# A scan and gated-MLP kernel: four of the first block's twelve hidden units move from whole fp32 products to three rounded passes, with a new start and load order

## The chip, the core and the metric

The kernel runs on one core of a Trainium2 chip. The metric is device time in microseconds (us): the median of the runs before the change is 351.71 us (351.47 to 352.11, 3 runs).

## What is computed

The first half is a gated linear scan over 768 positions for 4 batches and 8 heads, in chunks with decays that are products of `clip(a, 1e-6, 1)`. Its output, 3072 tokens of 256 features, goes through a gated MLP with 1536 hidden units:

```python
def _attn_ref(x, a, B, C):                 # (4,8,768,32), (4,8,768), (4,8,768,16) twice
    log_a = np.log(np.clip(a, 1e-06, 1.0))
    for c in range(nc):
        cum = np.cumsum(la, axis=-1)
        L = np.exp(cum[:, :, :, None] - cum[:, :, None, :]) * causal
        M = np.einsum('bhin,bhjn->bhij', Cc, Bc) * L
        y_intra = np.einsum('bhij,bhjd->bhid', M, xc)
        y_inter = np.einsum('bhin,bhnd->bhid', Cc, state) * np.exp(cum)[:, :, :, None]
        y[:, :, sl] = y_intra + y_inter
        state = decay_full[:, :, None, None] * state + np.sum(Bx, axis=2)
def _moe_ref(x, w_gate, w_val, w_out):
    g = x @ w_gate
    silu = g * (1.0 / (1.0 + np.exp(-g)))
    return (silu * (x @ w_val) @ w_out).astype(np.float32)
```

The reference's MLP runs in float64, since the weights come as float64: each arrives as two 32-bit words, and the kernel rounds it to fp32 itself.

## The kernel before, in words

**Blocks and stages.** The 768 positions are cut into 6 blocks of 128 (`NB`), each with all 4 batches: 512 tokens (`T`). Per block k there are three stages. *Scan*: the decay matrix `L` is built by scans on VectorE (DVE), the scores `S` on TensorE (PE) are mixed into it, then come values, states and carried values, which end in the tiles `y`. *Gate and value*: 12 units (`NF`) of 128 hidden features; unit f has two 128x512 results on PE, `gv` for gate and value, from the weight tile `wg{f}`; ScalarE (ACT) takes the silu, DVE the product `sg`. *Projection*: `hh`, a rounded high and a low part of `sg`, is multiplied with `wo`.

**Two kinds of product.** A rounded product (type fp32r) is done in three passes: high weight by high x, low weight by high x, high weight by low x (`xh`, `xl`, `wg..h`, `wg..l`), 12 matmuls a unit. Block 0's units are done instead as whole fp32 products, 4 instructions a unit, from `xf` (a plain copy of `y`) and the rounded weight `wg..w`, so that no high and low parts are needed yet.

**Weights.** A tile's way: `w_fetch` (SP's queue, into `wg..r`, 8 buffers), `w_magnitude` and `w_rest` (ACT), `w_range` (GpSimd, called POOL, for most tiles), `w_shift`, `w_sign`, `w_round` (DVE; the last is shown as ISA or CUSTOM_DVE_ANT_0). After that the whole products of block 0 can run. For block 1 ACT casts the high part (`w_high`) and writes the negated weight into the low part (`w_minus`), and a transfer issued by POOL adds the weight onto it (`w_low`, with `accum_op`). The `wo` tiles take their low part by a subtraction on DVE.

**Block 0's start.** The decays of block 0 come as few rows (`rows`), are clipped on DVE (`clip_rows`), spread to 128 partitions by products with `pick` on PE (tiles `a`), and scanned on DVE with the matrix `dj`, which is 1 where a partition's own position begins. `dj` is copied by ACT from the constant tile `cs`, which a transfer loads. Later blocks read their rows, clipped by POOL (`clip_all`), from `clipped` in DRAM.

**What sets the order.** All engines run in program order. That order is made when the kernel is built, by `Plan`: each step is added with its engine, a cost, a rank, what it needs, and the slots it takes; `order` picks, for the engine that can start first, the step of the lowest rank. `follow` fixes a sequence of steps. Every instruction is recorded by one helper, so all have the line L191 in the profile and are told apart by tiles.

## Time and profile before

| | us |
|---|---|
| median of 3 runs | 351.71 (351.47 to 352.11) |
| the profiled execution | 352.14, its span 350.3 |
| TensorE (PE) busy | 342.8, 98% of the span |
| VectorE (DVE) busy | 231.3, 66% |
| ScalarE (ACT) busy | 121.9, 35% |
| GpSimd (POOL) busy | 46.0, 13% |

A row of an engine's instructions in order of time gives start, length, engine, line, operation, output tile <- inputs, shape and count; in brackets stands how long the engine was idle before it and what ended that. PEld is PE's weight load, which overlaps PE. Busy shares are averages over stages: DVE is full in the first 60 us and half empty later.

### The profile page before, as it was taken

The numbers are of one execution on the slowest core, as the hardware profiler recorded it, in microseconds if no ns is written. First come the engines' busy times: TensorE is split into PE (matmuls) and PEld (weight loads), VectorE is DVE, ScalarE is ACT, GpSimd is POOL, SyncE is SP. The second block draws the span as 40 slices with busy tenths as digits, with TensorE's granted clock in tenths as the row PEclk, the third lists the DMA queues.
The fourth block names the chain that finished last, engine by engine and source line by source line (L and its number), as shares of the span: only waits on it lengthen the run. The fifth ranks groups of instructions, "written<-read, shape, count | busy, mean of one in ns | idle before, by whom it ended". The sixth has DMA issues, their size and how long they took to land.

```text
span 350.3 us, 7386 instructions
## 1 busy us (share of the span) xinstructions
PE 342.8 (98%) x3183; PEld 265.6 (76%) x3184; DVE 231.3 (66%) x415; ACT 121.9 (35%) x221; POOL 46.0 (13%) x36
## 2 busy tenths in 40 slices
PE   7999989999999999999999999999999999999996
PEld 5644445688878888878888878888888888888895
DVE  4999999998689774686447677456676430565320
ACT  3599677434355512212222222221212221222221
POOL 1374884402301000000000000000000000000000
PEclk9999999999999999999999999999999999999999
DMA  7799998850000751000382000281000000100001
GB/s 258 241 318 309 334 277 185 225 120 2 1 2 4 204 158 62 0 2 2 111 175 82 0 2 2 84 199 59 24 3 2 2 2 0 60 2 0 0 2 60
DMA packets 10216, 31.28 MB, mean 89 GB/s; under 512 B 1184, under 2 KB 2080, under 8 KB 9544
## 3 DMA queue, kind: packets, MB, share of 16 engines
q1 hardware_dynamic: 8136, 26.77, 25.4%
q0 software_dynamic: 1728, 3.15, 5.0%
q10 hardware_dynamic: 320, 0.89, 0.8%
q8 instruction: 25, 0.41, 0.5%
q14 instruction: 7, 0.06, 0.1%
HBM read 24.32 MB, written 3.35 MB: 79 GB/s over the span
## 4 chain that ended last, share of the span: by engine, by line
PE 92%; DVE 3%; issue 1%; ACT 0%; DVEq 0%; ACTq 0%
PE gv L191 57%; PE po L191 28%; PE y L191 5%; PE S L191 2%; DVE wg8w L191 1%; DVE L L191 1%; DVE wg0w L191 1%; DVE E L191 0%; DVE wg7w L191 0%; DVE sg L191 0%; DVE xb L191 0%; ACT ob L191 0%; DVE bc L191 0%; DVEq L191 0%; ACTq L191 0%
## 5 line engine op out<-in xcount | busy, mean ns | idle before, releaser
L191 DVE TENSOR_TENSOR sg<-gv,sg 128x512 f32<-128x512 f32 x72 | 49.5, 688 | 66.5 <-PE gv L191 65.3
L191 ACT ACTIVATE sg<-gv 128x512 f32<-128x512 f32 x72 | 43.1, 598 | 109.7 <-PE gv L191 109.6
L191 DVE TENSOR_TENSOR hh<-sg,hh 128x512 fp32r<-128x512 f32 x72 | 49.5, 691 | 16.0 <-ACT hh L191 14.6
L191 ACT CAST hh<-sg 128x512 fp32r<-128x512 f32 x36 | 22.3, 623 | 31.1 <-PE po L191 17.5
L191 DVE TENSOR_TENSOR_SCAN L<-L,dj 128x520 f32<-128x520 f32 x20 | 23.9, 1228 | 5.8 <-DMA L<-clipped 5.8
L191 ACT COPY ob<-po 128x512 f32<-128x512 f32 (+1 forms) x13 | 7.2, 555 | 48.6 <-PE po L191 48.2
L191 DVE CAST hh<-sg 128x512 fp32r<-128x512 f32 x36 | 15.8, 438 | 1.2
L191 PE MATMUL po<-hh,wo4h 128*128 128x512 f32 (+1 forms) x52 | 15.2, 375 | 0.0
L191 PE MATMUL po<-hh,wo2h 128*128 128x512 f32 (+1 forms) x52 | 15.2, 375 | 0.0
L191 PE MATMUL po<-hh,wo0h 128*128 128x512 f32 (+1 forms) x52 | 15.2, 375 | 0.0
L191 DVE TENSOR_TENSOR L<-S,L 128x512 f32<-128x512 f32 x24 | 15.1, 678 | 0.0
L191 PE MATMUL po<-hh,wo5h 128*128 128x512 f32 (+1 forms) x52 | 15.1, 373 | 0.0
L191 PE MATMUL po<-hh,wo1h 128*128 128x512 f32 (+1 forms) x52 | 15.0, 373 | 0.0
L191 PE MATMUL po<-hh,wo3h 128*128 128x512 f32 (+1 forms) x52 | 15.0, 373 | 0.0
L191 PEld LDWEIGHTS y<-L,xb 64*32 64x32 f32 x768 | 9.6, 111 | 3.1 <-issue 1.8
L191 PE MATMUL y<-L,xb 64*32 64x64 f32 x768 | 11.9, 239 | 0.0
L191 PEld LDWEIGHTS po<-hh,wo0h 128*128 128x128 f32 x52 | 9.5, 188 | 1.9 <-issue 0.2
L191 PEld LDWEIGHTS po<-hh,wo5h 128*128 128x128 f32 x52 | 9.5, 188 | 1.7
L191 PEld LDWEIGHTS po<-hh,wo1h 128*128 128x128 f32 x52 | 9.5, 188 | 1.7
L191 PEld LDWEIGHTS po<-hh,wo3h 128*128 128x128 f32 x52 | 9.5, 188 | 1.7
L191 PEld LDWEIGHTS po<-hh,wo2h 128*128 128x128 f32 x52 | 9.4, 188 | 1.8
L191 PEld LDWEIGHTS po<-hh,wo4h 128*128 128x128 f32 x52 | 9.4, 188 | 1.7
(304 smaller groups left out, 756.0 us busy)
## 6 DMA issues: line engine op xcount, KB each, us to landing
L<-clipped SPq DMA_DIRECT2D x10, 520.0 KB, 10.7
xb<-in_xb SPq DMA_DIRECT2D x5, 768.0 KB, 13.8
bc<-in_bc SPq DMA_DIRECT2D x6, 512.0 KB, 4.4
out<-ob SPq DMA_DIRECT2D x11, 256.0 KB, 2.0
E<-clipped SPq DMA_DIRECT2D x5, 260.0 KB
xb<-in_xb ACTq DMA_DIRECT2D x1, 768.0 KB, 6.3
wg0r<-in_wgv SPq DMA_DIRECT2D x1, 512.0 KB
wg1r<-in_wgv SPq DMA_DIRECT2D x1, 512.0 KB
```

The lines of the kernel that those rows point to most:

```text
L191: ins = getattr(self.engine, name)(*a, **k)
```

## The change

- `WHOLE = 8`: block 0's units 0 to 7 stay whole, units 8 to 11 are done in three rounded passes. Their weights' low parts are subtracted on DVE, as for the `wo` tiles, and are needed already in block 0.
- Block 0 gets an `xh` and an `xl`: ACT casts `xf` to `xh` and writes the negated `xf` to `xl`, in two halves each, and one transfer issued by POOL adds `xf` onto `xl`.
- `dj` is no longer made from `cs`: POOL counts positions into a tile `step` (IOTA, two halves), and DVE compares them with 0.
- `xb` of block 0 is loaded over SP's queue, behind `bc`; all four copies to `xf` are on ACT.
- The plan's lags, the conditions of the weight fetches (`HELD`) and a fixed order of loads (`ORDER`) are new; the slots `x` are split into `xh` and `xl`.

```diff
@@ -222 +222,2 @@
-    eye, hm, blk = cs[:, 0:W], cs[:, W : W + 2], cs[:, W + 2 : W + 2 + 2 * D]
+    hm, blk = cs[:, :2], cs[:, 2 : 2 + 2 * D]
+    step_of = const.tile([P, W], F32, name="step")
@@ -288 +289 @@
-        (sp if k else se).dma_start(t, xb[k])
+        sp.dma_start(t, xb[k])
@@ -523,0 +525,9 @@
+    def first_high(g, e):
+        copy(e, xh[0][:, g], whole[0][:, g])
+
+    def first_minus(g):
+        se.activation(xl[0][:, g], whole[0][:, g], AF.Copy, scale=-1.0)
+
+    def first_low():
+        ge.dma_start(xl[0], whole[0], accum_op=ALU.add)
+
@@ -588 +598 @@
-        if i < NF:
+        if i < WHOLE:
@@ -604 +614 @@
-        if not k:
+        if not k and f < WHOLE:
@@ -667 +677 @@
-        times, wide = (4, 64) if not n else (1, 512)
+        times, wide = ((4, 64), (1, 512))[n]
@@ -680,0 +691,6 @@
+    for q in range(K):
+        ge.iota(
+            step_of[piece(q)], pattern=[[1, W]], base=0, channel_multiplier=-1,
+            allow_small_or_imprecise_dtypes=True,
+        )
+    ve.tensor_scalar(dj, step_of.unsqueeze(1).to_broadcast([P, H, W]), 0.0, None, ALU.is_equal)
@@ -690 +706 @@
-        dict(mm=4, at=4, L=1, E=1, bc=1, xb=1, Cz=1, T=2, raw=RAW, w=1, x=2, sg=SG, ob=2),
+        dict(mm=4, at=4, L=1, E=1, bc=1, xb=1, Cz=1, T=2, raw=RAW, w=1, xh=2, xl=2, sg=SG, ob=2),
@@ -712 +727,0 @@
-    add([("Act", 0.6), ("DVE", 0.6)], None, lambda e: copy(e, dj, eye.unsqueeze(1).to_broadcast([P, H, W])), -8.5, ["cs"], gives="dj")
@@ -725 +740 @@
-        add("SP", 0.48, do(w_fetch, i), r - 9.0, [("S", 0, BATCH - 1)] if i in (2, 3) else [("M", 0, 2 * i - 7)] if i in (4, 5) else [("y", 0)] if i == 7 else [], takes=[("raw", ("raw", i))], gives=("raw", i), lag=2.1)
+        add("SP", 0.48, do(w_fetch, i), r - 9.0, [("S", 0, BATCH - 1)] if i == HELD else [], takes=[("raw", ("raw", i))], gives=("raw", i), lag=1.3)
@@ -727 +742 @@
-        far = not 0 < i < 3
+        far = i in FAR
@@ -730 +745 @@
-        add("Act", 0.57, do(w_rest, i, "Act"), r - 4.5, [("raw", i)], gives=("rest", i))
+        add("Act", 0.57, do(w_rest, i, "Act"), r - 4.5, [("raw", i), *([("xf", 3)] if i == 3 else [])], gives=("rest", i))
@@ -734 +749 @@
-        if i < NF:
+        if i < WHOLE:
@@ -738 +753 @@
-        if i < NF:
+        if i < WHOLE:
@@ -740 +755 @@
-            add("Pool", 1.2, do(w_low, i), r - 2.5, [("wh", i), ("minus", i), *whole_done], uses=[("w", i)], gives=("wl", i), slack=4.0)
+            add("Pool", 1.2, do(w_low, i), r - 2.5, [("wh", i), ("minus", i), *whole_done], uses=[("w", i)], gives=("wl", i), lag=3.0)
@@ -747 +762 @@
-    add("SP", 0.48, write_all, -9, ["clipped"], gives="written", lag=0.9)
+    add("SP", 0.48, write_all, -9, ["clipped"], gives="written", lag=1.5)
@@ -767,2 +782,2 @@
-        add(*q, load(load_bc), FETCH["bc"] if k == 1 else z - 7 if k else -7.7, late + behind("bc") + loaded, takes=[("bc", BC)], gives=("bc", k), lag=2.1)
-        add(*q, load(load_xb), FETCH["xb"] if k == 1 else z - 6 if k else -6, late + behind("xb") + loaded, takes=[("xb", XB)], gives=("xb", k), lag=3.1)
+        add(*q, load(load_bc), FETCH["bc"] if k == 1 else z - 7 if k else -7.7, late + behind("bc") + loaded, takes=[("bc", BC)], gives=("bc", k), lag=1.3)
+        add(*q, load(load_xb), FETCH["xb"] if k == 1 else z - 6 if k else -6, late + behind("xb") + loaded, takes=[("xb", XB)], gives=("xb", k), lag=1.9)
@@ -770 +785 @@
-            add("-", 0.0, lambda: None, -9, takes=[("x", "rows")], gives="rows", lag=0.2)
+            add("-", 0.0, lambda: None, -9, takes=[("xl", "rows")], gives="rows", lag=0.2)
@@ -778 +793 @@
-                    need = [t, ("decays", 0), "dj"] + ([("scan0", b)] if i else [])
+                    need = [t, ("decays", 0)] + ([("scan0", b)] if i else [])
@@ -783 +798 @@
-            add("SP", 0.48, do(load_an, k), FETCH["an"] if k == 1 else z - 9, ["written", ("decays", k), *late], gives=("an", k), lag=1.1)
+            add("SP", 0.48, do(load_an, k), FETCH["an"] if k == 1 else z - 9, ["written", ("decays", k), *late], gives=("an", k), lag=2.4)
@@ -831 +846,7 @@
-            add("-", 0.0, new_whole, -9, [("clip", 2)], takes=[("x", "xf")], gives="xf")
+            add("-", 0.0, new_whole, -9, [("clip", 2)], takes=[("xl", "xf")], gives="xf")
+            add("-", 0.0, do(new_x, 0), due(0, WHOLE) - 9, [("xf", i) for i in range(2 * K)], takes=[("xh", ("xh", 0)), ("xl", ("xl", 0))], gives=("x", 0))
+            for g in range(2):
+                r = due(0, WHOLE) - 7 + 2 * g
+                add("Act", 0.57, do(first_high, g, "Act"), r, [("x", 0)], gives=("xh", 0, g))
+                add("Act", 0.57, do(first_minus, g), r + 0.5, [("x", 0)], gives=("minus", "x", g))
+            add("Pool", 1.2, first_low, due(0, WHOLE) - 4.5, [("minus", "x", g) for g in range(2)], uses=["xf"], gives=("xl", 0, 0), lag=3.0)
@@ -833 +854 @@
-                add([("Act", 0.36)] if i < 3 else [("Act", 0.36), ("DVE", 0.36)], None, do(x_whole, i), -1 + i / 10, [("vals", i) if i < 2 else ("y", 0), "xf", *([("round", 0)] if i == 3 else [])], uses=[y[i]], gives=("xf", i))
+                add([("Act", 0.36)], None, do(x_whole, i), -1 + i / 10, [("vals", i) if i < 2 else ("y", 0), "xf"], uses=[y[i]], gives=("xf", i))
@@ -835 +856 @@
-        add("-", 0.0, do(new_x, k), z + 15, [("x", k - 1)] if k > 1 else ["xf"], takes=[("x", ("x", k))], gives=("x", k))
+        add("-", 0.0, do(new_x, k), z + 15, [("x", k - 1)], takes=[("xh", ("xh", k)), ("xl", ("xl", k))], gives=("x", k))
@@ -842 +863 @@
-        xs = [(t, k, i) for t in ("xh", "xl") for i in range(2 * K)]
+        xs = [(t, k, i) for t in ("xh", "xl") for i in range(2 * K if k else 2) if k or t == "xh" or not i]
@@ -847 +868,2 @@
-            if not k:
+            x = [("xh", k), ("xl", k)]
+            if not k and f < WHOLE:
@@ -849,0 +872 @@
+                x = ["xf"]
@@ -852 +875 @@
-                add("PE", c, do(gate_val, k, f, m), r + m * 0.1, need, takes=[("mm", gv[m])], uses=[gv[m], ("x", k) if k else "xf"], gives=gv[m], kind="r")
+                add("PE", c, do(gate_val, k, f, m), r + m * 0.1, need, takes=[("mm", gv[m])], uses=[gv[m], *x], gives=gv[m], kind="r")
@@ -881 +904,2 @@
-    plan.follow([("L", 0, b) if i else ("scan0", b) for b, i in halves] + [("M", 0, p) for p in range(3)] + [("bt", 0)] + [("M", 0, 3), ("E", 0), ("ce", 0), ("sign", 0)])
+    plan.follow(ORDER)
+    plan.follow([("L", 0, b) if i else ("scan0", b) for b, i in halves] + [("bt", 0)] + [("M", 0, p) for p in range(NP)] + [("E", 0), ("ce", 0), ("sign", 0), ("round", 0)])
@@ -886 +910 @@
-CST = W + 2 + 2 * D
+CST = 2 + 2 * D
@@ -891,0 +916,3 @@
+HELD = 2
+WHOLE = 8
+FAR = [0, *range(3, 18)]
@@ -892,0 +920 @@
+ORDER = [("raw", 7), "written", ("raw", 8), ("bc", 1), ("aj", 1), ("xb", 1), ("raw", 9), ("an", 1), ("raw", 10)]
@@ -925 +952,0 @@
-    cst[:, :W] = (p % Q)[:, None] == np.arange(W)[None, :]
@@ -927,2 +954,2 @@
-    cst[:, W : W + 2] = odd[:, None] == np.arange(2)[None, :]
-    cst[:, W + 2 : W + 2 + 2 * D] = odd[:, None] == (np.arange(2 * D) // D)[None, :]
+    cst[:, :2] = odd[:, None] == np.arange(2)[None, :]
+    cst[:, 2 : 2 + 2 * D] = odd[:, None] == (np.arange(2 * D) // D)[None, :]
```

At POOL's start, before (`ISA` there is the build's load of POOL's code library, put ahead of the first instruction of POOL that is not a memset):

```order
L191 MEMSET unit 128x384
L191 MEMSET dn 128x520
L191 MEMSET dn 128x8
L191 ISA
L191 TENSOR_SCALAR all<-all 128x6x64
```

and now:

```order
L191 ISA
L191 IOTA step 64x65 x2
L191 MEMSET unit 128x384
L191 MEMSET dn 128x520
L191 MEMSET dn 128x8
L191 TENSOR_SCALAR all<-all 128x6x64
```

The load of the library has moved ahead of the memsets, and the IOTA pair stands behind it.

At DVE's start, the difference up to the second scan:

```order
 L191 MEMSET unit 128x128
 L191 MEMSET warm 128x1
+L191 TENSOR_SCALAR dj<-step 128x520
 L191 TENSOR_SCALAR rows<-rows 8x8x64 x2
-L191 SCALAR_TENSOR_TENSOR L_95<-a_0_141,dj 128x260
-L191 SCALAR_TENSOR_TENSOR L_95<-a_0_146,dj 128x260
```

DVE now makes `dj` ahead of the clips of the rows, which stay ahead of the scans.

On DVE around the units that change (`L<-S` is a mix of block 1's scores, `T` a state), before, from wg9's rounding on:

```order
L191 ISA wg9w<-wg9r,wg9w 128x1024
L191 TENSOR_SCALAR wg10w<-wg10w 128x512
L191 SCALAR_TENSOR_TENSOR wg10w<-wg10r,wg10w 128x512
L191 TENSOR_TENSOR sg_8_646<-gv_8_1_642,sg_8_646 128x512
L191 ISA wg10w<-wg10r,wg10w 128x1024
```

and now, from wg9's low part on:

```order
L191 TENSOR_TENSOR wg9l<-wg9w,wg9h 128x512
L191 TENSOR_SCALAR wg10w<-wg10w 128x512
L191 TENSOR_SCALAR wg11w<-wg11w 128x512
L191 SCALAR_TENSOR_TENSOR wg10w<-wg10r,wg10w 128x512
L191 SCALAR_TENSOR_TENSOR wg11w<-wg11r,wg11w 128x512
L191 TENSOR_TENSOR sg_8_677<-gv_8_1_669,sg_8_677 128x512
L191 ISA wg10w<-wg10r,wg10w 128x1024
L191 TENSOR_TENSOR T_114<-y_2_684,cs 128x256
L191 ISA wg11w<-wg11r,wg11w 128x1024
L191 SCALAR_TENSOR_TENSOR T_114<-T_113,E_377,T_114 128x64 x4
L191 TENSOR_TENSOR wg10l<-wg10w,wg10h 128x512
```

Between wg9's rounding and wg10's stood three steps; between wg9's low part and wg10's there are now nine rows, wg11's steps among them.

## The prediction

> **What bounds the kernel now.** I read the waits of TensorE (PE) first, then busy time by stretches, then the engines' instructions in order of time up to the end of the first token block, and the chain of waits last. Units and weight tiles are counted from 0, so the change's units 9 to 12 are wg8 to wg11.

> The waits, as microseconds in total, times and the longest:

> ```profile
> PE a L191 <- DVE rows L191: 1.4, 1, 1.4
> PE gv L191 <- DVE wg8w L191: 1.2, 1, 1.2
> PE gv L191 <- DVE wg0w L191: 0.4, 1, 0.4
> ```

> All of PE's waits lie in the first block; behind it PE runs without a gap. So what counts is when PE starts block 1 (first product gv<-xh), and the rest of the span moves with that. PE in order of time (start, length), and three pieces of the chain of waits:

> ```profile
> 1.06 1.46 PE L191 MATMUL rest<-unit 128*128 128x64 bf16 x24 [1.06 <-DVE warm L191]
> 3.93 4.28 PE L191 MATMUL a<-rows,pick 8*128 8x260 f32 x16 [1.40 <-DVE rows L191]
> 8.13 2.30 PE L191 MATMUL S<-Cz,bc 32*64 32x128 f32 x64
> 10.36 1.23 PE L191 MATMUL a<-rows,pick 8*128 8x260 f32 x2
> 16.89 3.67 PE L191 MATMUL gv<-xf,wg0w 128*128 128x512 f32 x8 [0.40 <-DVE wg0w L191]
> 20.40 3.60 PE L191 MATMUL gv<-xf,wg1w 128*128 128x512 f32 x8
> 23.83 3.60 PE L191 MATMUL gv<-xf,wg2w 128*128 128x512 f32 x8
> 37.66 1.21 PE L191 MATMUL S<-Cz,bc 32*64 32x128 f32 x64
> 64.40 1.03 PE L191 MATMUL gv<-xh,wg0h 128*128 128x512 f32 x2
> ...
> 50.75 1.64 PE y L191 x105
> 57.73 1.88 PE y L191 x117
> 135.37 16.32 PE gv L191 x72
> ```

> Block 1 starts at 64.40. A whole fp32 unit takes 23.83 - 20.40 = 3.43 us, a rounded one 16.32 / 6 = 2.72.

> The second bound is VectorE (DVE). From the end of wg0's rounding to the start of wg11's last step it is busy 39.95 of 40.36 us (start:end, length, busy PE, PEld, DVE, ACT, POOL):

> ```profile
> 16.65:57.01 40.36, 38.97 (x275) 18.04 (x276) 39.95 (x70) 33.37 (x61) 30.00 (x20) 1.00 1.04 305
> ```

> PE and DVE are both full there. Work taken from PE and given to DVE is no gain by itself.

> **The change part by part.** *Passes.* Four units lose 3.43 - 2.72 each: 4 x 0.71 = 2.84 us less PE. If PE alone counted, the time from wg0's rounding (call it D0, 16.65 before) to block 1 would be 0.24 + 8 x 3.43 + 4 x 2.72 + 1.21 + 1.64 + 1.88 = 43.3, against 64.40 - 16.65 = 47.75 now.

> *DVE's load.* The costs, as steps from one start to the next:

> ```profile
> 16.05 0.69 DVE L191 CUSTOM_DVE_ANT_0 wg0w<-wg0r,wg0w 128x1024 uint16<-128x1024 uint16 x1
> 20.68 1.22 DVE L191 SCALAR_TENSOR_TENSOR T<-T,E 128x64 f32<-128x64 f32 x4
> 21.83 0.68 DVE L191 TENSOR_TENSOR sg<-gv,sg 128x512 f32<-128x512 f32 x1
> 22.43 0.68 DVE L191 CUSTOM_DVE_ANT_0 wg2w<-wg2r,wg2w 128x1024 uint16<-128x1024 uint16 x1
> 32.53 2.36 DVE L191 TENSOR_TENSOR_SCAN L<-L,dj 128x520 f32<-128x520 f32 x2
> 34.81 0.66 DVE L191 TENSOR_TENSOR sg<-gv,sg 128x512 f32<-128x512 f32 x1
> ...
> 43.35 0.77 DVE L191 TENSOR_SCALAR wg8w<-wg8w 128x512 int32<-128x512 int32 x1
> 47.45 0.41 DVE L191 TENSOR_SCALAR wg9w<-wg9w 128x512 int32<-128x512 int32 x1
> ```

> 0.60 for a two-input 512-wide step (21.83 to 22.43), 1.15 for a long scan, 0.35 for a one-input step, 1.15 for the first four state steps and 0.79 for a later four. By DVE's order, between wg0's rounding and the start of wg11's last step stand now: 36 two-input steps (21.6), five scans (5.75), 16 one-input steps (5.6), four short weighings (0.85), the state steps (1.94): 35.7. The trace has 40.36, so 4.6 us are stretching: steps longer beside GpSimd (POOL), such as 0.77 against 0.41 for the same shift, the first beside this row.

> ```profile
> 43.23 1.91 POOL L191 TENSOR_SCALAR wg9w<-wg9w 128x512 f32<-128x512 f32 x1 [0.90 <-ACT wg9w L191]
> ```

> In the changed order wg10's low part, the last one that keeps PE waiting, is done after 40 two-input steps (24.0), five scans, 14 one-input steps (4.9), the weighings and the state steps: 37.4, plus stretching. POOL keeps its range steps and drops a transfer, so I take 4.0 of the 4.6 (bounds: none, and 5.5). That part is done at D0 + 41.4. PE then has 10 of 12 products of wg10 (2.27), the carried values (1.88) and wg11 (2.72): block 1 at D0 + 48.3, against D0 + 47.75 now: **0.5 us later**, not 2.84 earlier. The saved passes stand as PE idle, 48.3 - 43.3 = 5.0 us, in front of wg8 to wg10, where 1.2 stood. Without stretching it is D0 + 44.3 (3.5 earlier), with 5.5 D0 + 49.8 (2.0 later).

> *Adding transfer of x.* POOL issues it behind wg8's range step, 12 us or so behind D0, from the earlier loads. The nearest row is a 256 KB adding transfer:

> ```profile
> wg5l<-wg5w POOLq DMA_DIRECT2D x1, 256.0 KB, 11.4
> ```

> Twice that is 23 us: D0 + 35, while wg8's third pair comes at about D0 + 32. It would hold wg8 by 3 us, but wg10 waits for DVE until D0 + 41.4 anyway. I cost it at nothing; its cover is that wait, and 3 us stand if it goes. Copies and negations on ScalarE (ACT) cost nothing: ACT is busy 33.37 of 40.36.

> *Load order.* SP now fetches eight weight tiles ahead of the write of the clipped rows; block 1's bc and L come behind wg8's fetch, which waits for wg0's raw buffer, so for D0. L took

> ```profile
> L<-clipped SPq DMA_DIRECT2D x2, 520.0 KB, 12.9
> ```

> from issue to landing: D0 + 1.5 + 12.9 = D0 + 14.4. Its first scan comes behind 14.5 us of DVE work with 1.5 of stretching, D0 + 16. Cost nothing; the cover is those 1.6 us, and past them DVE, which binds, would pay each one.

> *The start.* Before, the matrix dj comes from a load and a copy on ACT, and the scans wait for it until 5.72. Now POOL makes its source (IOTA), and the load of POOL's code library, which stood behind its memsets, stands ahead of IOTA. DVE's dj step waits for IOTA, and behind that one instruction wait the clips of the rows, the spreads on PE, the scans: the whole block.

> ```profile
> 3.46 0.86 DVE L191 TENSOR_SCALAR rows<-rows 8x512 f32<-8x512 f32 x2 [2.45 <-DMA rows<-in_aj]
> 5.72 1.88 DVE L191 TENSOR_TENSOR_SCAN L<-a,dj 128x260 f32<-128x260 f32 x3 [1.40 <-ACT dj L191]
> ...
> 2.54 1.28 ACT L191 ACT_TABLE_LOAD   x1 [2.54 <-issue]
> ...
> 0.74 0.42 POOL L191 MEMSET unit<- 128x384 bf16 x1 [0.29 <-POOLq L934]
> 1.09 0.71 POOL L191 MEMSET dn<- 128x520 f32 x2
> 8.96 1.49 POOL L191 TENSOR_SCALAR all<-all 128x384 f32<-128x384 f32 x1 [7.16 <-DMA all<-in_an]
> ```

> No row shows the library load. It lies in the 7.16 us between 1.80 and 8.96, where POOL waited for data anyway: it takes between 0 and 7.16, hidden. The other row of an engine loading tables is ACT's 1.28. I take 5.7, three quarters of the way from 1.28 to 7.16, nearer to the gap that holds this very load. Then: 0.74 + 5.7 = 6.44; two IOTAs 0.4 (between a one-column memset, 0.1, and the row of 0.71); dj 0.5 (0.41 to 0.86 by its neighbours): 7.34; to the first spread 0.47 as before (3.46 to 3.93): 7.81. Eight spreads took 4.28 behind the warming products that ended at 2.52; the ninth alone took 1.16 (10.36 to 11.52). With PE idle for 5 us ahead of them I take 0.70 each (bounds 0.535 and 0.87, the latter 1.16 less 0.3 of latency): 13.4. Scores 2.30: 15.7. From there four mixes, the E scan, five steps for wg0, wg2 and bc, at the costs above, 5.5 with small waits: D0 = 21.2, **4.55 us later**. With a load of 0 the scores end as now, the weighing of xb is out of the way, and D0 = 16.1, 0.5 earlier; with 7.16 and slow spreads D0 = 24.7.

> [...]

> *Sum.* 4.55 + 0.5 = 5.1 us. The profiled run took 352.14 with a span of 350.3; this becomes 355.4. From the median 351.71: **356.8**.

> **The rivals.**

> *The library load is short, DVE still binds.* For it: no row shows a load at all. IOTA is ready by 1.5, D0 is 0.5 earlier, block 1 still 0.5 later from there: 351.7, no change.

> *The load is short and DVE keeps up* (the faster side). Place: the stretching beside POOL between D0 and wg10's low part. If earlier loads let POOL finish its range steps while DVE waits less, 2 us are left of 4.6: block 1 at D0 + 37.4 + 2.0 + 6.9 = 46.3, 1.45 earlier, and D0 0.5 earlier: 349.8. It decides below a stretching of 3.9 and a load under about 2 us. Against it: as many range steps of 1.9 us as before.

> *A middle load*, 2 to 4 us: the dj step ends at 3.6 to 5.6, the spreads start 0.2 to 2.2 late: 352.5 to 354.5.

> *The changed order does not lengthen DVE* because hidden-half steps leave it: against it, the count above (four low parts more, and hh_0 is split earlier).

> **How the numbers follow.** Long load 0.60, its own range 354.0 to 360.4 (load of 4 with 0.6 us spreads and little stretching; the full gap with half-speed spreads); middle load 0.08; short load with DVE binding 0.14; short load and DVE keeping up 0.18. The predicted time is that of the first, 356.8. A measurement of this kernel tells 0.2%, 0.7 us, from no change: below 351.0 is faster, 0.18 and a little of the third case: 0.20; within, 0.09; slower 0.71. The range 350.3 to 360.2 leaves out most of the fastest case and the top of the longest load, some 0.17.

> **What would show each step.** POOL's IOTA at 6 to 7 us and DVE's dj step released by POOL behind it: the load is long; IOTA near 1 us: the forecast falls to about 351.7. Spreads spaced 0.53 or 0.87. wg0's rounding ending near 21. PE idle of several us in front of the groups that read wg8l and wg10l, released by DVE: DVE binds; none there: the 2.84 is real. The third pair of wg8 (gv<-xl) waiting for a DMA: the adding transfer is late. Block 1 starting 48.3 behind D0. The forecast is wrong if IOTA comes early, or if DVE shows gaps in the 40 us behind D0.

## The result, and the profile after

| | us |
|---|---|
| before, median of 4 runs | 351.9 (351.47 to 352.11) |
| after, median of 4 runs | 357.2 (355.1 to 358.2) |
| ratio, 95% interval | 1.0145 (1.0098 to 1.0192) |
| the profiled execution after | 358.2, its span 356.4 (before 350.3) |

The change makes the kernel 5.3 us slower; 356.8 was forecast. The time came out, but the larger of the forecast's two terms did not happen, and a cost that it does not have stands in its place. Where one execution of a kernel ran some per cent longer than its others, the medians and ratios below leave it out. The waits of TensorE (PE) in the changed kernel, as microseconds in total, times and the longest:

```profile
PE y L191 <- issue: 6.5, 2, 4.0
PE a L191 <- DVE rows L191: 1.3, 1, 1.3
PE gv L191 <- DVE wg8l L191: 0.6, 1, 0.6
PE gv L191 <- ACT sg L191: 0.4, 1, 0.4
```

The first row is new. Twice PE stands still in front of a small matmul of `y`, 6.5 us in all, and the row names no engine and no transfer of data: "issue" is a wait for nothing that the profile shows. The changed kernel's PE in order of time (start, length, then in brackets the idle time before and what ended it) shows where:

```profile
12.07 0.97 PE L191 MATMUL y<-L,xb 64*32 64x64 f32 x50
15.56 1.39 PE L191 MATMUL y<-L,xb 64*32 64x64 f32 x77 [2.52 <-issue]
18.77 3.75 PE L191 MATMUL gv<-xf,wg0w 128*128 128x512 f32 x8 [0.22 <-DVE wg1w L191]
...
52.77 0.99 PE L191 MATMUL y<-L,xb 64*32 64x64 f32 x61
57.72 0.31 PE L191 MATMUL y<-L,xb 64*32 64x64 f32 x1 [3.96 <-issue]
57.97 1.22 PE L191 MATMUL gv<-xh,wg9h 128*128 128x512 f32 x2
58.98 1.05 PE L191 MATMUL gv<-xh,wg9l 128*128 128x512 f32 x2
...
63.25 0.67 PE L191 MATMUL gv<-xh,wg10h 128*128 128x512 f32 x2
...
70.87 0.61 PE L191 MATMUL gv<-xh,wg0h 128*128 128x512 f32 x2
```

Both stops lie in the middle of a run of equal matmuls: 50 of them went, the next 77 had the same inputs. Behind the second stop a pair of 128x512 products takes 1.05 us instead of 0.62, so wg9 takes 63.25 - 57.97 = 5.28 us and not the 2.72 of a rounded unit. Block 1 starts at 70.87; before it was 64.40. These 6.47 us are the whole loss (the span grew by 6.1).

The start of the changed kernel, on GpSimd (POOL) and VectorE (DVE):

```profile
0.85 0.42 POOL L191 IOTA step<- 64x65 f32 x2 [0.40 <-POOLq L961]
1.30 1.20 DVE L191 TENSOR_SCALAR dj<-step 128x520 f32<-128x520 f32 x1 [0.29 <-POOL step L191]
5.07 1.88 DVE L191 TENSOR_TENSOR_SCAN L<-a,dj 128x260 f32<-128x260 f32 x3 [0.88 <-PE a L191]
```

IOTA runs at 0.85 us and the first scan starts at 5.07, before at 5.72. The long library load of the forecast is not there. (The first scan is now released by the spread tile `a`, no longer by `dj`.)

DVE's own list, at the end of wg0's rounding (D0) and around wg10's low part:

```profile
17.39 0.68 DVE L191 CUSTOM_DVE_ANT_0 wg0w<-wg0r,wg0w 128x1024 uint16<-128x1024 uint16 x1
17.99 0.42 DVE L191 TENSOR_SCALAR wg2w<-wg2w 128x512 int32<-128x512 int32 x1
...
58.64 0.68 DVE L191 TENSOR_TENSOR wg10l<-wg10w,wg10h 128x512 fp32r<-128x512 f32 x1
59.24 0.86 DVE L191 SCALAR_TENSOR_TENSOR T<-T,E 128x64 f32<-128x64 f32 x4
63.55 0.69 DVE L191 TENSOR_TENSOR sg<-gv,sg 128x512 f32<-128x512 f32 x1 [3.44 <-ACT wo2r L191]
```

D0 is 17.99, and wg10's low part is done at 59.24, so D0 + 41.25. Of these 41.25 us DVE is busy 39.44; 1.81 it idles at 28 to 30 us, for a range step of wg6 on POOL that takes 4.99 there. Behind wg10's low part DVE idles 3.44 us; the row names ACT, but the product it starts with needs wg9, which PE ends only at 63.25.

**What the stops wait for.** The profile's list of DMA queues has one that carries no data of the kernel: q8, "instruction". In the changed kernel, over the whole span and then in the stretch 13.1 to 14.4 us (packets, MB, share of 16 engines):

```profile
q8 instruction: 25, 0.41, 0.5%
...
q8 instruction: 1, 0.02, 5.2%
```

25 packets of 0.41 MB are 16 KB each. PE's matmuls and its weight loads (PEld), from the page's list of engines:

```profile
PE 343.0 (96%) x3199; PEld 270.3 (76%) x3200; DVE 231.0 (65%) x417; ACT 122.7 (34%) x223; POOL 46.2 (13%) x35
```

```profile
8.00:13.00 5.00, 4.96 (x131) 3.48 (x130) 5.00 (x9) 1.24 (x2) 3.41 (x2) 1.00 0.52 197
```

and after:

```profile
8.00:13.00 5.00, 5.00 (x182) 3.79 (x181) 4.96 (x9) 2.89 (x6) 3.40 (x2) 1.00 1.02 416
```

Before, wg2r stood behind the write of `clipped` in SP's queue, which waits for POOL's clipping until about 10.5 us: the queues ran empty. After, six more weight tiles stand ahead of that write, and a 16 KB packet has to come through queues that keep the DMA engines at 1.02 instead of 0.52.

### The profile page after: what moved, and what is told of

It reads as the page before. It is cut to its first block, busy times and chain, and to the rows that moved or that the text cites. A ratio compares the mean times of both kernels' runs of the same rounds, so it can differ in the third digit from the quotient of the medians.

```text
span 356.4 us, 7415 instructions
## 1 busy us (share of the span) xinstructions
PE 343.0 (96%) x3199; PEld 270.3 (76%) x3200; DVE 231.0 (65%) x417; ACT 122.7 (34%) x223; POOL 46.2 (13%) x35
## 4 chain that ended last, share of the span: by engine, by line
PE 91%; DVE 4%; issue 3%; DMA 1%; ACT 0%; DVEq 0%; ACTq 0%
PE gv L191 55%; PE po L191 28%; PE y L191 5%; PE S L191 2%; DVE L L191 2%; PE a L191 2%; DMA rows<-in_aj 1%; DVE wg8w L191 0%; DVE wg7w L191 0%; DVE E L191 0%; PE st L191 0%; DVE xb L191 0%; DVE wg9w L191 0%; DVE wg2w L191 0%; DVE wg8l L191 0%
## 5 line engine op out<-in xcount | busy, mean ns | idle before, releaser
L191 DVE TENSOR_TENSOR sg<-gv,sg 128x512 f32<-128x512 f32 x72 | 49.5, 687 | 73.9 <-PE gv L191 69.6
L191 ACT ACTIVATE sg<-gv 128x512 f32<-128x512 f32 x72 | 43.2, 600 | 115.3 <-PE gv L191 115.2
L191 DVE TENSOR_TENSOR hh<-sg,hh 128x512 fp32r<-128x512 f32 x72 | 49.7, 695 | 12.2 <-ACT hh L191 10.6
L191 ACT CAST hh<-sg 128x512 fp32r<-128x512 f32 x32 | 19.8, 622 | 28.1 <-PE po L191 16.2
L191 DVE TENSOR_TENSOR_SCAN L<-L,dj 128x520 f32<-128x520 f32 x20 | 24.6, 1249 | 7.5 <-DMA L<-clipped 7.5
L191 ACT COPY ob<-po 128x512 f32<-128x512 f32 (+1 forms) x13 | 7.2, 555 | 48.7 <-PE po L191 48.2
L191 DVE CAST hh<-sg 128x512 fp32r<-128x512 f32 x40 | 17.1, 427 | 2.4 <-PE po L191 1.2
L191 PE MATMUL y<-L,xb 64*32 64x64 f32 x768 | 11.8, 239 | 6.5 <-issue 6.5
L191 PEld LDWEIGHTS y<-L,xb 64*32 64x32 f32 x768 | 9.6, 112 | 8.7 <-issue 8.7
L191 PE MATMUL po<-hh,wo4h 128*128 128x512 f32 (+1 forms) x52 | 15.2, 375 | 0.0
L191 PE MATMUL po<-hh,wo2h 128*128 128x512 f32 (+1 forms) x52 | 15.2, 375 | 0.0
L191 PE MATMUL po<-hh,wo0h 128*128 128x512 f32 (+1 forms) x52 | 15.2, 375 | 0.0
L191 PE MATMUL po<-hh,wo5h 128*128 128x512 f32 (+1 forms) x52 | 15.1, 373 | 0.0
L191 PE MATMUL po<-hh,wo3h 128*128 128x512 f32 (+1 forms) x52 | 15.0, 373 | 0.0
L191 PE MATMUL po<-hh,wo1h 128*128 128x512 f32 (+1 forms) x52 | 15.0, 373 | 0.0
L191 DVE TENSOR_TENSOR L<-S,L 128x512 f32<-128x512 f32 x24 | 14.9, 682 | 0.0
L191 PEld LDWEIGHTS po<-hh,wo0h 128*128 128x128 f32 x52 | 9.5, 188 | 1.9 <-issue 0.2
L191 PEld LDWEIGHTS po<-hh,wo3h 128*128 128x128 f32 x52 | 9.5, 188 | 1.7
L191 PEld LDWEIGHTS po<-hh,wo5h 128*128 128x128 f32 x52 | 9.5, 188 | 1.7
L191 PEld LDWEIGHTS po<-hh,wo1h 128*128 128x128 f32 x52 | 9.5, 188 | 1.7
L191 PEld LDWEIGHTS po<-hh,wo2h 128*128 128x128 f32 x52 | 9.4, 188 | 1.8
L191 PEld LDWEIGHTS po<-hh,wo4h 128*128 128x128 f32 x52 | 9.4, 188 | 1.7
## 6 DMA issues: line engine op xcount, KB each, us to landing
out<-ob SPq DMA_DIRECT2D x11, 256.0 KB, 2.0
```

The source lines that it names most:

```text
L191: ins = getattr(self.engine, name)(*a, **k)
```

## The experiments

Three theories. **T1, late pages:** PE stops where the next page of its program has not come, and the page comes late because its packet stands behind full DMA queues. **T2, the place:** the stops belong to the place where a page ends in the program (a run of small matmuls, 50 in 0.97 us by the rows above), whatever the queues hold. **T3, DVE:** with no stop at all the saved passes would still be no gain, since PE would wait for DVE in block 0. All ratios are against the kernel before on the same chip.

### The load order alone

The kernel before with the changed SP order and the plan's lags that go with it, and nothing else; the edit in short:

```
-  wg2r, wg3r wait for S, wg4r, wg5r for M, wg7r for y (planner)
+  wg2r waits for S (HELD = 2)
+  plan.follow(ORDER)      # raw 7, "written", raw 8, bc 1, aj 1, ...
```

> The kernel before with one part of the change alone: the new load order (SP's queue holds wg0r to wg7r ahead of the write of the clipped rows, and the order of block 1's loads is that of the change). No unit has other passes, dj is read as before. Theory 1 (page packet behind full queues): the 16 KB packet that came at 11.1 us in the kernel before now comes behind the weights, at 13 to 14 us; a stop of 1.5 to 2.5 us on issue appears before PE's y near 15.5 us, and block 1 starts 1.5 to 2 us later: 353.2 to 354. Theory 2 (place in the program): the same PE instructions in the same places of the first block's start, no stop, 351.9 within 0.3. My prediction's price for the load order was nothing (351.9).

Measured: 356.96 us, ratio 1.0146 (1.0092 to 1.0201): the same loss as the whole change. PE in order of time, and then the busy times of 8 to 13 us:

```profile
16.11 0.35 PE L191 MATMUL st<-xb 64*32 64x64 f32 x7 [1.73 <-issue]
...
62.58 0.35 PE L191 MATMUL y<-bc,T 32*64 32x64 f32 x9 [1.11 <-issue]
```

```profile
8.00:13.00 5.00, 4.96 (x131) 3.38 (x130) 5.00 (x9) 2.49 (x4) 3.40 (x2) 1.00 1.03 415
```

The page's packet came at 13.54 us instead of 11.07. PE's list of instructions is that of the kernel before, but for wg1's and wg2's products, which changed places from 22 us on: T2 has no explanation for the first stop. The loss was larger than I expected (5.0 instead of 1.3 to 2): there are two further stops at page ends, 0.66 at the 1217th instruction and 1.11 at the 1473rd, the second row above. With the first they sum to 3.5 us, and block 1 starts 3.3 us late. 1.6 us more are lost inside block 1, of which waits for DVE's `sg` name 1.0.

### The rounding alone

The changed kernel with SP's order of before: IOTA, the three passes for wg8 to wg11 and the adding transfer of x stay. In short:

```
-  plan.follow(ORDER); wg2r waits for S (HELD = 2)
+  wg2r, wg3r wait for S, wg4r, wg5r for M, wg7r for y (planner)
```

> The changed kernel without its load order: IOTA, units 9 to 12 in three rounded passes, low parts on VectorE and the adding transfer of x stay; SP's queue is that of the kernel before (the write of the clipped rows ahead of wg2r). Theory 1: no stop before y at 15.6 us (the first one falls away, as in the run with the write first); a second one near 57 us may stay, since the adding transfers and the loads of wo go out as in the changed kernel: 351.5 to 355.5. Theory 2 (place in the program): both stops stay, 357. Theory 3 (DVE's ledger): where neither stop is left, wg10's low part on DVE ends about 41.3 us after the end of wg0's rounding (D0 near 16.1 to 16.6 us), PE waits for it 2 us or more, and the time is 351 to 352.5, not below 350.5. My prediction's long library load (4.55 us) would show as an IOTA at 6 us and D0 at 21 us; the changed kernel's profile has IOTA at 0.85 us already, so it should be at 0.9 here too.

Measured: 354.05 us, ratio 1.0075 (1.0037 to 1.0114). DVE, and then PE, each in order of time:

```profile
15.45 0.69 DVE L191 CUSTOM_DVE_ANT_0 wg0w<-wg0r,wg0w 128x1024 uint16<-128x1024 uint16 x1
...
54.10 0.69 DVE L191 TENSOR_TENSOR wg10l<-wg10w,wg10h 128x512 fp32r<-128x512 f32 x1
...
49.34 0.71 PE L191 MATMUL y<-L,xb 64*32 64x64 f32 x46 [2.64 <-DVE L L191]
49.98 1.22 PE L191 MATMUL gv<-xh,wg8h 128*128 128x512 f32 x2
51.00 1.05 PE L191 MATMUL gv<-xh,wg8l 128*128 128x512 f32 x2
...
54.36 0.62 PE L191 MATMUL gv<-xh,wg9h 128*128 128x512 f32 x2
...
64.64 0.62 PE L191 MATMUL gv<-xh,wg0h 128*128 128x512 f32 x2
```

No stop on issue is left. D0 is 15.45 + 0.60 = 16.05, 0.6 earlier than before, and block 1 starts at 64.64, 0.24 later than before, 48.6 behind D0. So T3 holds for this order of DVE's work: the 2.84 us of saved passes and the 0.6 of the earlier start went into a wait of 2.64 for DVE's mix of block 1's scores and into half speed behind it (the granted clock is 0.50 from 50 to 53 us, and wg8 takes 54.36 - 49.98 = 4.38 instead of 2.72). It is not wg10's low part that PE waits for: that is done at 54.10 + 0.60 = 54.70, only 38.65 behind D0, some 5 us before PE needs it at 59.61. The rest of the loss, 1.5 us by the spans (352.0 against 350.3), comes later: in the projection PE waits 1.2 us for wo5's high and low parts, behind a POOL range step of 4.2 us (1.9 before).

### The write of the clipped rows first

```
-ORDER = [("raw", 7), "written", ("raw", 8), ...
+ORDER = [("raw", 1), "written", ("raw", 2), ("raw", 8), ...
```

> The changed kernel with one edit: the write of the clipped rows stands again ahead of wg2r in SP's queue, so that the loads of wg2r to wg7r go out about 6 us later, as they did in the kernel before. Theory 1 (PE stops where a 256-instruction page of its own program has to come in, and that 16 KB packet stands behind full DMA queues): the DMA engines have idle time at 9 to 11 us again, the page's packet ends near 12 us and not 14.3 us, the stop of 2.52 us before PE's y at 15.56 us vanishes, gv of wg0w starts near 16.5 us and the time falls by about 2 us, to 355. The second stop (3.96 us at 57.7 us) stays. Theory 2 (the stop comes from the place of the page's end in the program, a fast stretch of small matmuls, whatever the queues hold): PE's program has the same places, so the stop stays at about 2.5 us and the time at 357. Theory 3 (DVE's ledger sets the end of block 0 in any case): D0, the end of wg0's rounding, falls with the stop, from 18.0 to about 16.1 us, and wg10's low part ends at D0 + 41 us.

Measured: 357.49 us, ratio 1.0146 (1.0086 to 1.0205), no better than the change; 355 was expected. The DMA engines were 0.64 busy instead of 1.02:

```profile
8.00:13.00 5.00, 5.00 (x196) 3.91 (x196) 4.97 (x9) 3.35 (x8) 3.88 (x2) 1.00 0.64 206
```

The packet ran from 9.89 to 10.83 us; the first stop is gone, with exactly the same list of PE instructions as in the changed kernel. That decides against T2 for this stop. But the 2 us did not arrive at the end. PE began wg0 at 17.62 instead of 18.77, held up by ACT's copy of x (ACT had stood before it in wait of wg2r, which this edit loads later), and behind that wait the clock was 0.50 for 3.4 us, so wg0 took 5.23 us instead of 3.59. And the second stop grew:

```profile
17.62 5.40 PE L191 MATMUL gv<-xf,wg0w 128*128 128x512 f32 x8 [2.08 <-ACT xf L191]
...
57.94 1.01 PE L191 MATMUL gv<-xh,wg9h 128*128 128x512 f32 x2 [5.07 <-ACT wg11h L191]
```

The last row names ACT and wg11h, which this product does not read. It is the same page end: PE passed its 961st instruction at 51.18, the packet ran from 55.64 to 56.62 with the DMA engines at 1.10, and PE went on 1.32 behind it.

### The loads of wo2 to wo5 later

```
+    plan.follow([("raw", 13), ("bc", 2), ("raw", 14)])
-LATE = {2: NF + 2}
+LATE = {2: NF + 1}
```

> The changed kernel with one edit: the loads of wo2r to wo5r stand behind the loads of block 2 in SP's queue, so that they go out after 57 us instead of at 44 to 52 us. Theory 1 (PE's page packet stands behind full DMA queues): with half of the traffic of 44 to 56 us gone, the packet that ended at 56.3 us in the changed kernel comes 2 us or more earlier, the stop of 3.96 us before PE's y at 57.7 us shrinks to under 2 us, the half clock behind it (2.6 us) shortens, and the time falls by 2 to 4 us, to 353 to 355. If the adding transfers of the low parts alone fill the queues, the stop shrinks by less than 1 us. Theory 2 (place in the program): the stop stays at about 4 us and the time at 357.

Measured: 353.17 us, ratio 1.0039 (1.0017 to 1.0061): some 4 us of the 5.3 are back, with the changed kernel's list of PE instructions. Busy times of 52 to 56 us, first of this run and then of the changed kernel, and this run's second stop:

```profile
52.00:56.00 4.00, 2.75 (x133) 2.34 (x113) 4.00 (x8) 2.38 (x6) 0.22 (x1) 1.00 0.43 77
```

```profile
52.00:56.00 4.00, 1.76 (x128) 1.48 (x127) 4.00 (x9) 1.26 (x4) 0.55 (x1) 1.00 1.05 293
```

```profile
54.69 0.24 PE L191 MATMUL y<-L,xb 64*32 64x64 f32 x1 [1.25 <-issue]
```

The packet started 0.62 us after PE passed the 961st instruction (3.21 in the changed kernel), the stop fell from 3.96 to 1.25, no half speed followed, and block 1 starts at 66.29.

### Both edits

> The changed kernel with two edits together: the write of the clipped rows ahead of wg2r, and wo2r to wo5r behind block 2's loads. Theory 1 (page packets behind full DMA queues): no stop before y at 15 us (packet near 10 us), at 53 us a stop of at most 1.5 us. Theory 3 (DVE's ledger sets the end of block 0 once PE isn't stopped): D0 near 16.1 us, wg10's low part ends near D0 + 41 = 57 us or where DVE's order ends it, PE waits for DVE 1 us or more ahead of block 1's y or of wg10, and block 1 starts at 64.0 to 65.0 us, level with the kernel before (64.4): 351.3 to 352.8 us. If the saved passes came through as a gain, block 1 would start at 61 to 62 us and the time would be 349 us. If the stops had another cause than the queues, they stay in sum over 4 us and the time is over 355.

Measured: 355.21 us, ratio 1.0093 (1.0068 to 1.0117). A miss: the first stop is gone (packet at 10.01), but the second is 3.47.

```profile
56.47 0.62 PE L191 MATMUL gv<-xh,wg9h 128*128 128x512 f32 x2 [3.47 <-issue]
56.92 0.62 PE L191 MATMUL gv<-xh,wg9l 128*128 128x512 f32 x2
```

Its packet came at 54.03, 2.71 after the crossing, with the DMA engines at 1.11. Of the bytes in 48 to 54 us none are weights any more: all are the adding transfers of POOL, which in this run fall later (in the run with late weights the DMA engines stood at 0.15 between crossing and packet). So either kind of traffic delays a page, and taking one away does not help where the other then falls on the page end. The time of a version depends on when it crosses its page ends as well as on its work.

### Page ends moved

16 fewer small matmuls and weight loads in PE's warm-up, so that all page ends fall 16 instructions later in the work.

```
-IDLE = [-9.0] * 6, [0.5, 1.0]
+IDLE = [-9.0] * 4, [0.5, 1.0]
```

> The changed kernel with one edit: 16 fewer small matmuls in PE's warm-up (8 instructions of two kinds each), so that every later page end falls 16 instructions further on in the work: the one of the second stop no longer at the last small matmul of block 1's y, but inside the large matmuls of wg9. Theory 1 (late packet): the packet still ends at 56 to 56.5 us; PE reaches the page's end only after several large matmuls (0.3 us each), so the second stop shrinks to under 2.5 us and less half clock follows: 354 to 356. The first stop stays at 2 to 2.8 us (the end falls 0.1 us later in the same run of small matmuls). Theory 2 (place alone): the first stop stays and the second goes entirely, time 352 to 353. If the packet is asked for by PE's progress and nothing else, the stop merely moves and keeps its 4 us: 357.

Measured: 354.07 us, ratio 1.0069 (1.0043 to 1.0094).

```profile
15.17 1.32 PE L191 MATMUL y<-L,xb 64*32 64x64 f32 x69 [2.20 <-issue]
...
56.97 0.50 PE L191 MATMUL gv<-xh,wg9h 128*128 128x512 f32 x1 [1.43 <-issue]
```

As T1 said: the first stop stays, the second lies now in a large matmul of wg9 and is 1.43. The place counts too, through the time at which PE gets there: PE goes on 1.3 to 1.5 us behind the packets' ends, as in the other runs. Part of the shrinkage is not the place: the second packet started 1.98 us after the crossing (3.21 in the changed kernel) and ended at 55.50, earlier than the 56 to 56.5 expected.

### The pages of all these runs

From the trace's records of q8 and of PE (us; "crossed" is when PE reached its 193rd or 961st instruction, one page ahead of the page that the packet is taken to bring, and every packet of these rows starts behind it; "DMA" is the engines' busy share from there to the packet's start):

| run | crossed | packet | DMA | PE goes on | stop |
|---|---|---|---|---|---|
| before, page from 449 | 9.61 | 11.07 to 12.00 | 0.22 | in time | 0 |
| after | 9.35 | 13.19 to 14.27 | 1.03 | 15.56 | 2.52 |
| load order alone | 9.75 | 13.54 to 14.65 | 1.03 | 16.11 | 1.73 |
| late wo | 9.35 | 12.48 to 13.57 | 1.03 | 15.00 | 1.97 |
| page ends moved | 9.36 | 12.81 to 13.87 | 1.03 | 15.17 | 2.20 |
| clipped first | 9.17 | 9.89 to 10.83 | 0.77 | in time | 0 |
| both edits | 9.42 | 10.01 to 10.96 | 0.59 | in time | 0 |
| after, page from 1217 | 52.11 | 55.32 to 56.29 | 1.06 | 57.72 | 3.96 |
| clipped first | 51.18 | 55.64 to 56.62 | 1.10 | 57.94 | 5.07 |
| both edits | 51.32 | 54.03 to 54.93 | 1.11 | 56.47 | 3.47 |
| page ends moved | 52.11 | 54.09 to 55.50 | 1.09 | 56.97 | 1.43 |
| late wo | 51.78 | 52.40 to 53.43 | 0.15 | 54.69 | 1.25 |

In these rows a packet starts 2.0 to 4.5 us after PE crosses where the DMA share is over 1, and 0.6 to 1.5 where it is under 0.8; it takes 0.9 to 1.4; and wherever PE stops it goes on 1.2 to 1.7 us behind the packet's end. T1 is shown, by kernels with equal PE programs whose stops come and go with the traffic; T2 alone is out.

Two limits of this rule. The share alone does not tell the delay: with two units in three passes (below) a packet came 0.77 us after the crossing at a share of 1.07, and the page from the 961st instruction came 11.7 us after PE's 705th in the changed kernel and 12.0 in the kernel before, which cost nothing, since PE was then in long fp32 products and needed that page only 14 us after its packet. And the crossing in PE's records is not itself what asks for the page: later, in long rounded products, the packet starts before it (at 84.23 in the kernel before, where PE reaches the 1729th instruction at 88.39).

### IOTA alone

The kernel before with `dj` made from IOTA (the six lines of the diff) and no other part. PE's list of instructions is that of before.

> The kernel before with one part of the change alone: IOTA and a comparison make dj, in place of the read of a constant and its spreading; every unit and load as before. My prediction's long library load (IOTA at 6.4 us, D0 4.55 us late) would give 356.3. The changed kernel's profile (IOTA at 0.85 us, first scan 0.65 us earlier) gives a D0 up to 0.65 us earlier; in block 0 of the kernel before PE is busy nearly throughout, so block 1 would start up to 0.6 us earlier: 351.2 to 351.9.

Measured: 351.52 us, ratio 0.9991 (0.9971 to 1.001).

```profile
0.85 0.42 POOL L191 IOTA step<- 64x65 f32 x2 [0.40 <-POOLq L939]
1.31 0.73 DVE L191 TENSOR_SCALAR dj<-step 128x520 f32<-128x520 f32 x1 [0.29 <-POOL step L191]
...
63.57 1.03 PE L191 MATMUL gv<-xh,wg0h 128*128 128x512 f32 x2
```

No library load, and in this profiled run block 1 is 0.8 us early (63.57). Over all runs that is not told from no change.

### Two units in three passes

> The changed kernel without its load order, with the three rounded passes for two units (wg10 and wg11) in place of four, and the range step of wo5 on VectorE in place of GpSimd (in the run with the rounding alone PE waited 1.2 us for wo5's low part and lost 1.6 us there). PE saves 1.42 us of passes instead of 2.84, DVE has two low parts (1.36 us) less before block 1. Theory 3 (DVE's ledger): the wait of 2.6 us for DVE before block 1's y that the rounding alone showed falls by about 1.4 us, block 1 starts at 62.9 to 64.4 us, and the time is 350.4 to 352.2. If DVE isn't what binds, the run loses the 1.4 us of passes that it gives back on PE and block 1 starts at 65.8 us or later: 353.4. Theory 1: no stop on issue of over 1 us before 70 us, with the loads of the kernel before.

Measured: 353.46 us, ratio 1.0051 (1.0034 to 1.0068), a miss against the 350.4 to 352.2 of theory 3. Block 1 starts at 64.25, as good as with four units (64.64), so half the saved passes are worth as much as all of them, nothing, which is T3's side; behind that PE waits 2.1 us for DVE's `hh` in the projection, which the planner's new order brought along. A stop of 0.51 us lies at the 1217th instruction, 1.49 behind its packet's end.

### DVE's order, to get the saved passes through

The rounding alone, with block 1's mixes ahead of wg8's low part on DVE, and wo5's range step on DVE:

```
+    plan.follow([*(("M", 1, p) for p in range(NP)), ("wl", 8), ("shift", 9)])
-FAR = [0, *range(3, 18)]
+FAR = [0, *range(3, 17)]
```

> The run with the rounding alone (units 9 to 12 in three passes, IOTA, the kernel before's load order), with DVE's order changed at one place: block 1's four products of scores and L stand ahead of wg8's low part and of wg9's steps, and wo5's range step is on VectorE. In the run with the rounding alone PE waited 2.64 us for the last of these products (46.7 to 49.3 us) and then worked at half clock to 53.2 us, about 2 us more. Theory 3 (the saved passes went into a wait for DVE's order and the half clock behind it): the wait shrinks to under 1 us, the granted clock stays 1.00 at 50 to 53 us, a smaller wait for wg9's low part appears, and block 1 starts at 62.5 to 64.0 us instead of 64.4; with the 1.6 us at wo5 gone too: 350.0 to 351.8. If DVE's total work binds whatever the order, block 1 starts at 64.4 us again and the time is 352.2 to 352.6.

Measured: 353.79 us, ratio 1.0057 (1.0032 to 1.0081), a miss. Its waits:

```profile
PE y L191 <- issue: 2.2, 1, 2.2
PE gv L191 <- issue: 0.9, 1, 0.9
PE y L191 <- DVE L L191: 0.7, 1, 0.7
PE gv L191 <- DVE wg9l L191: 0.4, 1, 0.4
```

The wait for the mix fell from 2.64 to 0.71 and the half speed is gone, as expected. But now the pages stop it: crossing at 45.63 with the packet at 49.21, crossing at 51.67 with the packet at 55.53, the DMA engines at 1.08 to 1.09, stops of 0.87 and 2.16. Between the two stops, at block 1's carried values, PE was at 54.9 us 3.1 us ahead of the run with the rounding alone, or 1.7 ahead in work, since half of wg9 (1.36 us) still lay before it that the other run had done; the second stop is longer than that lead, and block 1 starts at 65.4. A faster PE reaches its page ends earlier, and here its packets did not come earlier by as much.

With wg9's low part ahead of wg10's first step as well:

> The same, and wg9's low part also ahead of wg10's first step on DVE. Theory 3: as in the run with the products first, and the wait for wg9's low part shrinks by 1.4 to 2 us, so that block 1 starts at 62.0 to 63.5 us: 349.5 to 351.2. If DVE's total work binds whatever the order, the wait moves to wg10's or wg11's low part and block 1 starts at 64.4 us: 352.2 to 352.6. Theory 1: with the loads of the kernel before, a stop on issue can come back only where PE reaches a page's end earlier than the packet, near 54 to 58 us, with full queues from the adding transfers: up to 1.5 us.

Measured: 355.04 us, ratio 1.0089 (1.0054 to 1.0125), a miss. The waits for DVE fell to 0.9 us, and the stops grew to 0.96 and 2.70, the second followed by half speed (1.05 a pair).

With the first of these two orders and the loads of wo2 to wo5 late:

> The run with block 1's products first on DVE, with wo2r to wo5r behind block 2's loads as in the run with late weights (DVE's and PE's orders up to block 1 nearly those of the run with the products first, by extra order rules). There PE was 3.06 us ahead of the run with the rounding alone at block 1's carried values (54.9 us), and lost 0.87 us at 50.8 and 2.16 us at 56.0 us in stops on issue, at page ends, with full DMA queues; block 1 started at 65.1. Theory 1 (page packets behind full queues): with the loads of wo2r to wo5r gone from 44 to 57 us the packet that came 3.86 us after PE crossed the page's end comes in 0.6 to 1.5 us, the stop of 2.16 us falls to under 0.6 us, the one of 0.87 us stays or shrinks, and block 1 starts at 62.5 to 63.7 us; with no loss after it: 349.8 to 351.3, faster than the kernel before. If the stops had another cause they keep 3 us in sum, block 1 starts near 65 us and the time is 352.6 to 353.8.

Measured: 353.18 us, ratio 1.0043 (1.0024 to 1.0063), a miss in time. The packet came within 0.5 us of the crossing and the long stop is gone. But in this run PE got past block 1's mixes 2.2 us later: it waited 1.4 ("issue") and 1.1 us (DVE's mix) in front of and in block 1's values and 0.9 for wg9's low part, with half speed between, and block 1 starts later than in the run it was to improve. The first of these waits is put down to "issue", but no page end lies there. It ends at 47.13 us, 0.07 behind the end of DVE's first mix of block 1 (46.38 to 47.06), and this run's records have one sequencer wait fewer (31) than those of the run with the products first (32). So it was most likely the mix too, which comes later in this order of DVE; shown it is not.

Last, the run with the mixes first and page ends 36 instructions later (one 128-wide matmul in place of four 64-wide ones in the warm-up):

```
-        times, wide = ((4, 64), (1, 512))[n]
+        times, wide = ((1, 128), (1, 512))[n]
```

> The run with block 1's products first on DVE, with PE's first six rests made of one 128-wide matmul instead of four 64-wide ones: 36 PE instructions fewer ahead of the work, so every page end falls 36 instructions later in it, all else alike. There PE stopped 0.87 us at a page end in wg8's last matmuls and 2.16 us in block 1's carried values; a packet started 3.6 to 3.9 us after the crossing, took 0.9 to 1.0, and PE went on 1.3 to 1.7 us behind its end: about 6 us from crossing to page under full DMA queues. By this rule (theory 1): the first page end now falls 36 instructions later (wg9's first half and some small matmuls, 1.2 to 1.6 us of work), so its page is there in time and the stop of 0.87 us goes; PE crosses at about 52.5 us, the next page is there at 58.3 to 59 us, PE needs it at 57 to 57.6 us, in wg10's large matmuls, and stops 0.8 to 1.9 us there. Sum of stops 0.8 to 1.9 instead of 3.0 us; block 1 starts at 63.6 to 64.6 instead of 65.1 us; time about 1.3 us under the 353.8 of that run: 352.0 to 353.2. If the stops are bound to the kind of work (small matmuls of y), they stay at the same work and the time at 353.8.

Measured: 352.13 us, ratio 1.0016 (0.9996 to 1.0035); the ratio is 0.4% under that of the run it changes, with intervals that overlap. Its waits:

```profile
PE y L191 <- DVE L L191: 1.9, 2, 1.1
PE gv L191 <- DVE wg9l L191: 0.8, 1, 0.8
PE gv L191 <- ACT wg9h L191: 0.6, 1, 0.6
PE gv L191 <- issue: 0.3, 1, 0.3
```

The stops on issue fell from 3.0 to 0.3 us, the larger one to where it was expected, in wg10's products. In their place stand waits for DVE and ACT, 3.3 us instead of 1.1. In the two profiled executions block 1 starts at the same 65.4, not at the 63.6 to 64.6 expected; a gain is seen only in the medians. This is the best version with three passes, and it is level with the kernel before. None of the runs beats it beyond its interval. Whether the saved passes can be a gain, with neither stops at page ends nor waits for DVE, stays open: no run got rid of both.

## Why the prediction was right, and where it was wrong

**The time and its sign** came out (356.8 against 357.2), the forecast's likeliest mechanism did not; the agreement is luck. Point by point:

- **"The start"**: the step that failed first. The code-library load was put at 5.7 us, nearer to the 7.16 us gap that holds it, and D0 was to be 4.55 us late. IOTA stands at 0.85 us in the changed kernel, in the rounding alone and by itself, 0.40 behind the memsets of one column, and alone it costs nothing (351.52). The gap in which I placed the load was a wait for data: with the load gone from it, POOL still waits there until the same time (8.90 us, before 8.96). That a thing may hide in a gap is no sign that it has the gap's length. The other bound, a load of nothing with D0 at 16.1, is what the runs show (16.05 in the rounding alone); none shows the 5.7, which was my estimate.
- **"Load order. Cost nothing"**: the step that failed second, and where the time went. I followed the loads to those who read them (L, 1.6 us of cover) and not to the other users of the DMA engines. The load order alone costs 5.0 us, 3.3 of them ahead of block 1, through PE's pages, which the forecast does not mention at all.
- **"DVE's load"**: that the saved passes go into waits for DVE holds in the run with the rounding alone, the path does not. wg10's low part was put at D0 + 41.4. In the changed kernel it is done at D0 + 41.25, but with 1.81 us of DVE idle in it; in the rounding alone it is done at D0 + 38.65, and PE needs it 5 us later. In neither run does PE wait for it. Block 1 was put at D0 + 48.3, and the rounding alone has it at D0 + 48.6, by another sum: a wait of 2.64 for block 1's mix, not for wg8's and wg10's low parts, and 1.7 of half speed, where the forecast has 5.0 of idle time. So this agreement is chance too.
- **The sum**: 4.55 for the load that isn't there and 0.5 for DVE, against 1.34 at D0 and 5.13 from D0 to block 1 as measured. Counted where PE starts wg0 (18.77, before 16.89) it is 1.88 and, from there to block 1, 4.59. The first is the stop of 2.52 less the 0.6 gained at the start. The second is the stop of 3.96, 2.56 of half speed and waits of 0.57 and 0.42 for wg8's low part and for `sg`, less the 2.84 of saved passes and the 1.15 that PE waited for wg8 before: 3.52. The other 1.1 are not placed one by one; the rounded units wg10 and wg11 take 2.87 each instead of 2.72. That the forecast time and the measured one agree within 0.4 us is chance.
- **"Adding transfer of x"**: costed at nothing, and PE does not wait for it; it landed in 10.2 us in the changed kernel, not 23. But together with the others of its kind it fills the queues that PE's pages need (the DMA engines stood at 1.11 ahead of the late packet in the run with both edits, by adding transfers alone), which is a cost I did not look for.
- **The rival "load short, DVE still binds"**, 351.7 with a chance of 0.14, is nearest to what the runs show without the new load order: some 352.5, an estimate (the rounding alone less its 1.5 us at wo5). IOTA near 1 us was named as the sign that the long load is not there, and IOTA stands at 0.85.
- **"I take 0.70 each"**: no run shows the 5 us of idle time that this price of the spreads was taken for, nor the price; PE waited 1.1 to 2.0 us ahead of them, and in the changed kernel, after 1.28, eight took 4.28, 0.535 each, as before. The 0.3 of latency in the upper bound was my estimate. The clock column tells nothing at this place: the clock records begin at 15.90 us in the kernel before and at 18.96 in the changed one, and the column shows 1.00 where there is no record. That PE is slow there is seen in one product: `rest` with 128x512 takes 0.39 us at 16.10 in the kernel before and 0.61 at 17.94, still ahead of the first record, in the changed one.

**The page ends.** The trace shows the size of a page (25 packets of 16 KB for 6399 PE instructions, some 25 x 256) and its queue, q8. In the kernel before, PE's waits name DVE alone, so no page end shows as a stop; in the changed kernel two do, with 2.52 and 3.96 us.

## What to carry to other kernels

With many small instructions in a row PE ate its own program fast here (50 matmuls and as many weight loads in 0.97 us, so a page of 256 in 2.5 by estimate), and its next page came late where data kept the DMA engines full (2.0 to 4.5 us after the crossing in the table's rows with a share over 1): leave gaps in the traffic where such a run comes (late weights: 4 us back), or try to put a stretch of long instructions on that page, whose gain is shown here for one stop alone (3.96 to 1.43). An idle row that names "issue", or a tile that the instruction does not read, is to be laid beside the instruction queue's packets before it is laid to an engine. And when loads are moved, price them for everybody on the queues, not only for those who wait for the loaded data.

## What the hardware showed that was not expected

- The 16 KB instruction packets for which PE stopped had started 1.8 to 4.5 us after PE crossed a page end where the DMA engines were at 1.01 to 1.13 (once 0.77, at 1.07), and 0.62 after it where they were at 0.15. PE went on 1.2 to 1.7 us behind the packet's end in all 17 stops of ten runs.
- Half speed after a wait does not follow from the wait's length alone: 2.64 us were followed by 1.05 us a pair for three pairs, 3.96 by six, and 3.47 in the run with both edits by none (0.62 at once). In the clock records of the traces the half-speed stretches before 70 us last 3.41 or 6.83 us, twice that, and the full-speed stretches between them are multiples of 3.41 too (37.55 us, 11 times, ahead of the 6.83 in the changed kernel). Laid on this grid, five windows of 3.41 us at full speed with 2.03 to 2.75 us of PE idle in them were followed by half speed, and none with 1.56 or less; 1.90 was, and 1.91 in the run with both edits was not, where the 3.47 fell on two windows.
- A new order of loads alone cost 5.0 us, 3.3 of them before block 1; the longest wait of PE in the first block of the kernel before is 1.4 us.
